# Score visits that wait for each bank pair on its own, and a down-projection in 512 columns

## The chip, the cores and the metric

The kernel runs on one core of a Trainium2 chip. The metric is device time in microseconds (us), the median of several executions. Engines are named as in the profile: PE is TensorE's matmuls and PEld its weight loads, DVE is VectorE, ACT is ScalarE, POOL is GpSimd, SP is SyncE, which issues the DMAs.

## The reference

One transformer block over x of 2048 tokens by 1024 features: attention with 32 query heads of width 32 that share one key and one value head, then a gated feed-forward part of width 3584, each behind a layer norm and with a residual.

```python
q = (ln(x) @ wq) as 32 heads of 32;  k = ln(x) @ wk;  v = ln(x) @ wv
p = softmax(q k^T * 32**-0.5)            # no mask: 2048 x 2048 for each head
h = x + concat_heads(p @ v) @ wo
g, u = ln(h) @ w_gate, ln(h) @ w_up      # 3584 columns each
out = h + (sigmoid(g) * u) @ w_down
```

All inputs and the output are bf16. `ln` is a layer norm without scale or shift.

## The kernel before

**A planner writes the order.** The kernel's Python first builds a plan. Class `Plan` keeps a list of operations for each engine, with an estimate of when each is ready, how long it holds its engine (`occ`) and when its result is there (`lat`, or for a DMA an estimate from its bytes and a constant, `late`). TensorE's list is written by one loop that looks, at each estimated moment, for what is ready. The other engines take the ready operation with the best priority. The lists are then emitted as they stand; real semaphores guard each true dependence, and a wait is left out when the engine has already waited for as high a value. So an engine runs its list strictly in order, whatever the real times are. The dictionary `TUNE` holds the constants of the planner: `late` and `pace` for DMAs, `parts1` for the number of attention parts of the second half tile, `eb` and `eq` for the choice between ACT and DVE when a result leaves PSUM, `pv_few` and `d_off`, `d_b` for when attention and down-projection work may be taken up.

**Score visits.** Attention goes over half tiles `hf` (128 tokens and 16 heads; 32 of them) and key tiles `kt` (128 keys; 16 of them): 512 visits, numbered v. In a visit four matmuls run in four row strips of the array at once (K is 32), each of 512 columns (4 heads by 128 queries), into four PSUM banks of `S_ps`. Those six banks are three pairs, used in rotation. Two exps follow on ACT, numbered u = 2v and 2v+1, each over 1024 columns of one pair, into a half of a slot of `Pr` (L701 in the profile). A visit v writes the pairs that exps 2v-3 and 2v-2 have read. `s_ready` gives what a visit waits for, `emit_S` writes it, and `choose` picks the half tile in the first 32 visits. Before the change all four matmuls wait for exp 2v-2, which comes after 2v-3 on the same engine, and both exps wait for the last of the four matmuls:

```python
            if v >= 1:
                deps.append(exps[2 * v - 2])
```

**The rest of the attention.** `mk_PV` multiplies the exps by V, in column strips of the array: a round of four matmuls (four groups of heads) runs at once, and 16 key tiles make 16 rounds for a half tile, in two or more parts. DVE adds each part into `oun` (L797, L801) and adds the exps up in `acc` (L676); `mk_SUM` sums those over the keys, and the reciprocal goes out to DRAM and comes back spread over the partitions (`rb`). `mk_OP` is the output projection, 16 matmuls a tile.

**The feed-forward part** of a tile of 128 tokens: `mk_GU`, seven groups of 512 columns, each one gate group and one up group of 8 matmuls into one bank of `F_ps`; a tanh on ACT (L983) and a product on DVE (L1004) make the activation, which a DMA transposes into `hact`. `mk_D` is the down-projection, 28 matmuls (3584 = 28 x 128) for each slice of the 1024 output columns. With `nd=4` there are four slices of 256 columns for each tile; DVE adds each slice to the residual (L1051). Gate and up weights are streamed from DRAM again for each tile, in slabs of 1 MB, into a ring of four slabs. For the first and the last tile the weights are the stationary side, and the matmuls have 128 columns.

All matmul groups other than the visits share the two banks of `F_ps`; a group can start when the eviction of the group before it in that bank is done. A visit is put between the matmuls of such groups whenever `s_ready` says it can begin and ACT has less than `run` = 700 ns of work left. The array has three modes here: row strips (visits), column strips (attention times V, sums) and dense (the rest). On DVE, short evictions have priority over the adds of L676.

Nearly all matmuls have the line number L445, that of a helper, so the profile tells them apart by their tiles: `S_ps<-QTb,kT` is a visit, `F_ps<-Pr,Vt` is exp times V, `F_ps<-acc,sel` a sum, `F_ps<-ring,hnT` gate or up, `F_ps<-zone,hact` the down-projection, `F_ps<-wo_sb,OT` the output projection.

Of the kernel before, what the change touches and what calls it, by code (L numbers as in the profile page):

```python
# [9 lines left out]
ACTF = mybir.ActivationFunctionType  # L10
# [5 lines left out]
SEM = 75.0  # L16


TUNE = dict(look=500, ln_v=1, warm=70, late=400, ws0=1, ws1=1, parts0=3, parts1=3, lord=2, h_ord=2, ho=3,
            ho2=0, pvl1=0, pvl2=0, col_ok=0, pace0=310, swait=400, parts=2, raw=1, rl=0, nd=4, pc=16, rate=315,  # L20
            pace=250, xd=4, qf=1, dall=1, wo_late=1, nkn=3, few=0, rmin=900, hmin=1, h0=100, h1=250, hf=1.35,
            run=700, sum_few=0, pv_few=3, d_off=1, d_a=-1, d_b=0, eb=700, eq=400)


class Op:
# [16 lines left out]
class Plan:  # L42
# [53 lines left out]
    def start_of(self, o):  # L96
# [4 lines left out]
        if o.eng == "dve" and o.prio >= 6:  # L101

            for p in self.heap["dve"]:
                if p.prio < 6 and s < p.ready < s + TUNE["look"]:
                    return p.ready
        return s

    def step(self, limit):
# [21 lines left out]
        if o.nbytes:  # L130
            if o.pace:
                self.pace_free = s + o.nbytes / TUNE["pace0" if self.fast(s) else "pace"]
            k = o.key.rstrip("0123456789_")
            go = max(s + 1720.0, self.dma_free)
            w = self.SLOW.get(k, 1.0) if k != "ha" else 2.5 if o.nbytes < 200000 else 1.3
            self.dma_free = go + o.nbytes * w / TUNE["rate"]
            o.end = self.dma_free + 700.0 + self.LATE.get(k, 0.0) + TUNE["late"]
        else:
# [20 lines left out]
def t_act(n):  # L159
    return dict(occ=n / 1.2 + 58.0, lat=n / 1.2 + 186.0 + SEM)  # L160
# [9 lines left out]
def bass_sequential_preLN__grouped_kv_mqa__glu_gated_glu__prompt_kernel(  # L170
# [19 lines left out]
    SCALE = 1.0 / math.sqrt(DH)  # L190
# [11 lines left out]
    with ExitStack() as es:  # L202
# [66 lines left out]
        pl = Plan()  # L269
# [45 lines left out]

        for c in ["xxqxxqxxxxxxqxxxxq", "qxqxxqxqxxxxxxxxxx", "xqxqxqqxxxxxxxxxxx", "xqxqxqxqxxxxxxxxxx", "xxqxqxqxqxxxxxxxxx"][TUNE["lord"]]:
            if c == "x":
# [19 lines left out]
        def stats(ph, tiles, srcs, deps, prio, after=((), ())):  # L337
# [8 lines left out]
            for t, src, dp in zip(tiles, srcs, deps):  # L346
# [14 lines left out]
                      occ=90, lat=250)  # L361
            if ph and TUNE["ln_v"] or not ph and t0 < 2:

# [80 lines left out]
        def mm(o, l, r, start, stop, **kw):  # L444
            return lambda: PE.matmul(o, lhsT=l, rhs=r, start=start, stop=stop, **kw)  # L445

        def pe_op(fn, n, mode, deps, last_of_round=True):
            if mode != pl.pe_mode:
                pl.free["pe"] += SWITCH
                pl.pe_mode = mode  # L450
            if mode == "dense":
                occ = max(25.0, n / 2.4 + 2.4)
            else:
                occ = max(25.0, n / 2.4 + 2.4) - 10.5 if last_of_round else 3.5
            return pl.op("pe", fn, deps, occ=occ, lat=max(25.0, n / 2.4 + 2.0) + 170.0 + SEM)
# [171 lines left out]
        def choose(v, t):  # L627

            cand = sorted((nxt[h], h) for h in range(2) if nxt[h] < NT)
            for kt, h in cand:  # L630
                visits[v] = (h, kt)
                sd = s_ready(v)
                if sd is not None and known(sd, t):
                    return
            visits[v] = cand[0][::-1]

        exps = {}
# [9 lines left out]
        def s_ready(v):  # L647
            hf, kt = visits[v]
            c, hh = hf // 2, hf % 2
            if any(2 * hh + k not in q_ready[c] for k in range(2)) or kt not in k_ev or not free_slots:  # L650
                return None
            deps = [q_ready[c][2 * hh], q_ready[c][2 * hh + 1], k_ev[kt]]
            if v >= 1:
                deps.append(exps[2 * v - 2])
            return deps

        late_adds = collections.defaultdict(list)
        RAW = tuple(range(TUNE["raw"])) + ((NH - 1,) if TUNE["rl"] else ())
# [2 lines left out]
        def make_add(hf, kt):  # L661

            pred = hf - 2
            if pred >= 0 and pred not in RAW and pred not in sum_last:
                late_adds[hf].append(kt)
                return
            a = acc[:, hf % 2, :]
            slot = slot_of[(hf, kt)]
            dp = [exp_of[(hf, kt, i)] for i in range(2)]
            if kt == 1:  # L670
                in0 = slot_of[(hf, 0)]
                dp += [exp_of[(hf, 0, i)] for i in range(2)] + [sum_last.get(pred)]
            else:
                in0 = a
                dp.append(add_op[(hf, kt - 1)])
            add_op[(hf, kt)] = pl.op("dve", lambda: DVE.tensor_tensor(out=a, in0=in0, in1=slot, op=ALU.add), dp, prio=6,  # L676
                                     occ=1135, lat=1255)
# [5 lines left out]
        def emit_S(v):  # L683
            hf, kt = visits[v]
            c, hh = hf // 2, hf % 2
            if hf < 2:
                nxt[hf] += 1
            deps = s_ready(v)
            last = None
            for j in range(4):  # L690
                bank = 2 * ((2 * v + j // 2) % NB) + j % 2
                last = pe_op(mm(S_ps[:, bank, :], kT4[DH * j:DH * (j + 1), kt * P:(kt + 1) * P],
                                QTb[DH * j:DH * (j + 1), (c // 2) % 2, 4 * hh:4 * hh + 4, (c % 2) * P:(c % 2 + 1) * P],
                                True, True, tile_position=(DH * j, 0)),
                             512, "row", deps if j == 0 else [], j == 3)
            slot, rel = free_slots.popleft()
            slot_of[(hf, kt)] = slot
            for i in range(2):
                u = 2 * v + i
                pb = 2 * (u % NB)  # L700
                exps[u] = pl.op("act", lambda i=i, pb=pb: ACT.activation(  # L701
                    out=slot[:, i * 1024:(i + 1) * 1024].rearrange("p (a b) -> p a b", a=2), in_=S_ps[:, pb:pb + 2, :],
                    func=ACTF.Exp, scale=SCALE), [last] + rel, prio=3, **t_act(1024))
                exp_of[(hf, kt, i)] = exps[u]
            if kt >= 1 and hf not in RAW:
                make_add(hf, kt)
            if hh == 1 and c % 2 == 1 and kt == NT - 1:
                pair_last_S[c // 2] = last
                load_q(c // 2 + 2)
            if kt + 1 in parts_of(hf):  # L710
                if kt == NT - 1 and hf not in RAW:
                    queues["SUM"].append(mk_SUM(hf))
                queues["PV"].append(mk_PV(hf, parts_of(hf).index(kt + 1) - 1))
                if hf in RAW:
                    queues["PV"].append(mk_PV(hf, parts_of(hf).index(kt + 1) - 1, True))
# [3 lines left out]
        def parts_of(hf):  # L719
            return PARTS[TUNE["parts" if hf > 1 else "parts0" if hf == 0 else "parts1"]]  # L720
# [353 lines left out]
        cur = None  # L1074
        cur_i = 0
        cur_b = None
        v = 0
# [3 lines left out]
        def all_done(v):  # L1081

            v_done[0] = v
            if v == NV:
                all_S[0] = True
                pl.t_last = pl.free["pe"]
                load_next([(s.rearrange("p (d f) -> p d f", d=4), rel) for s, rel in free_slots])

        def known(deps, t):
            return all(d is not None and d.end is not None and d.end <= t for d in deps)  # L1090

        while True:
            t = pl.free["pe"]
# [14 lines left out]
            if v < NV:  # L1108
                run = max(pl.free["act"], t) + sum(o.occ for o in pl.heap["act"])
                if v < 2 * NT:  # L1110
                    choose(v, t)
                sd = s_ready(v)
                can_s = sd is not None and known(sd, t)
                if can_s and run - t < TUNE["run"]:
                    emit_S(v)
                    v += 1
                    all_done(v)
                    idle = 0
                    continue
                if pl.pe_mode == "col" and sd is not None and not can_s and not (  # L1120
                        cur is not None and cur[1][cur_i][2] != "dense") and known(sd, t + TUNE["swait"]) and run - t < TUNE["run"] + TUNE["swait"]:

                    pl.free["pe"] = t + 25.0
                    continue
            else:
                can_s = False
            if cur is not None and not held and cur[0].cls in LONG and known(bank_rel[1 - cur_b], t):

                for cl in ("PV", "SUM", "OP", "hT"):
                    if queues[cl] and (v >= NV or len(free_slots) <= TUNE["few"] or cl == "PV" and pl.pe_mode == "row" or (  # L1130
                            len(cur[1]) - cur_i) * max(25.0, cur[1][cur_i][1] / 2.4 + 2.4) >= TUNE["rmin"]):
                        gr = queues[cl][0]
                        if (gr.gate is None or gr.gate()) and known(gr.first(), t):
# [3 lines left out]
                            cur = (gr, gr.atoms(cur_b), list(bank_rel[cur_b]) + gr.first())  # L1137
                            cur_i = 0
                            break
            if cur is not None:  # L1140
                at = cur[1][cur_i]
                if known(at[3], t):
# [7 lines left out]
                    if cur_i == len(cur[1]):  # L1150
                        bank_rel[cur_b] = cur[0].after(cur_b, o)
                        cur = None
                        if held:
                            cur, cur_i, cur_b = held.pop()
                    idle = 0
                    continue
            else:
# [14 lines left out]
                if pick is not None:  # L1172
# [4 lines left out]
                    cur = (gr, gr.atoms(b), list(bank_rel[b]) + gr.first())  # L1177
                    cur_i, cur_b = 0, b
                    continue
            if can_s:  # L1180
                emit_S(v)
                v += 1
                all_done(v)
                continue
# [113 lines left out]
```

## Time and profile before

| | |
|---|---|
| time, median of 3 | 1097.02 us (1096.5 to 1098.07) |
| span of the profiled execution | 1098.3 us |
| granted TensorE clock | 0.998 of full speed |
| exps: 1024, mean length | 949.3 us busy for 1008 of them, 1120 ns each |
| tanhs: 112 | 75.4 us, 673 ns each |
| down-projection matmuls: 1792 | 224.3 us, 273 ns each |
| gate and up matmuls of 512 columns: 1439 recorded | 357.5 us, 380 ns each |

How to read it: an engine's instructions overlap, the end of one with the start of the next, so the mean length of one is not the spacing between two. An exp lasts 1120 ns and yet 1008 of them are busy for 949.3 us in all. Spacing is read from starts in the timeline. Some matmul records are missing in the trace, so a count of 1439 stands for more.

### The profile page before, as it was taken

The numbers are of one execution on the slowest core, as the hardware profiler recorded it, in microseconds if no ns is written. First come the engines' busy times: TensorE is split into PE (matmuls) and PEld (weight loads), VectorE is DVE, ScalarE is ACT, GpSimd is POOL, SyncE is SP. The second block draws the span as 40 slices with busy tenths as digits, with TensorE's granted clock in tenths as the row PEclk, the third lists the DMA queues.
The fourth block names the chain that finished last, engine by engine and source line by source line (L and its number), as shares of the span: only waits on it lengthen the run. The fifth ranks groups of instructions, "written<-read, shape, count | busy, mean of one in ns | idle before, by whom it ended". The sixth has DMA issues, their size and how long they took to land.

```text
span 1098.3 us, 25235 instructions
## 1 busy us (share of the span) xinstructions
PE 1062.8 (97%) x10227; PEld 529.1 (48%) x10350; DVE 851.6 (78%) x1087; ACT 1003.4 (91%) x1151; POOL 39.5 (4%) x61
## 2 busy tenths in 40 slices
PE   7999989999999999999999999999999999999999
PEld 6533465444444444444444444444444444444598
DVE  7988988787878878787878878787887878787311
ACT  4999999999999999999999999999999999999010
POOL 3300000000000000000000000000000000000000
PEclk9999999999999999999999999999999999999999
DMA  8793598958869595968868595877859595886993
GB/s 247 146 319 97 134 309 274 271 140 259 224 177 255 141 271 145 258 174 241 235 167 257 141 267 151 257 190 213 254 148 260 136 259 155 245 216 176 284 310 109
DMA packets 296515, 233.80 MB, mean 213 GB/s; under 512 B 99536, under 2 KB 282832, under 8 KB 296400
## 3 DMA queue, kind: packets, MB, share of 16 engines
q1 hardware_dynamic: 296400, 232.19, 76.1%
q8 instruction: 82, 1.34, 0.5%
q14 instruction: 33, 0.27, 0.1%
HBM read 203.82 MB, written 8.12 MB: 193 GB/s over the span
## 4 chain that ended last, share of the span: by engine, by line
PE 46%; ACT 42%; issue 4%; DVE 4%; DMA 3%; SPq 1%; POOL 0%; DVEq 0%
PE F_ps L445 39%; ACT Pr L701 38%; PE S_ps L445 7%; ACT tnh L983 3%; DVE acc L676 2%; DMA rb<-r_scratch 1%; DMA ring<-in_A_x_dram 1%; DMA ring<-in_B_w_up_dram 1%; SPq L303 0%; SPq L745 0%; DMA r_scratch<-r_sb 0%; ACT hact L701 0%; ACT QTb L701 0%; DVE h_sb L1051 0%; SPq L312 0%
## 5 line engine op out<-in xcount | busy, mean ns | idle before, releaser
L701 ACT ACTIVATE Pr<-S_ps 128x1024 bf16<-128x1024 f32 x1008 | 949.3, 1120 | 4.6 <-PE S_ps L445 4.4
L676 DVE TENSOR_TENSOR acc<-acc,Pr 128x2048 bf16<-128x2048 bf16 x430 | 524.6, 1220 | 72.3 <-ACT Pr L701 59.8
L445 PE MATMUL F_ps<-ring,hnT 128*128 128x512 bf16 x1439 | 357.5, 380 | 11.2 <-issue 9.2
L445 PE MATMUL F_ps<-zone,hact 128*128 128x256 bf16 x1792 | 224.3, 273 | 0.1
L445 PEld LDWEIGHTS F_ps<-ring,hnT 128*128 128x128 bf16 x1536 | 131.4, 97 | 176.2 <-issue 58.6
L445 PE MATMUL S_ps<-QTb,kT 32*128 32x512 bf16 x2048 | 202.4, 385 | 8.2 <-ACT Pr L701 2.9
L445 PEld LDWEIGHTS F_ps<-zone,hact 128*128 128x128 bf16 x1792 | 166.3, 98 | 51.9 <-issue 21.1
L445 PEld LDWEIGHTS S_ps<-QTb,kT 32*128 32x128 bf16 x2048 | 51.5, 91 | 183.5 <-ACT Pr L701 141.8
L445 PE MATMUL F_ps<-Pr,Vt 128*32 128x512 bf16 x2016 | 136.2, 382 | 0.0
L983 ACT ACTIVATE tnh<-F_ps 128x512 f32<-128x512 f32 x112 | 75.4, 673 | 61.0 <-PE F_ps L445 44.8
L1004 DVE SCALAR_TENSOR_TENSOR act_s<-tnh,F_ps 128x512 bf16<-128x512 f32 x98 | 67.0, 684 | 24.1 <-PE F_ps L445 23.6
L445 PE MATMUL F_ps<-zone 128*128 128x512 bf16 (+3 forms) x573 | 73.8, 272 | 6.0 <-DMA zone<-in_A_wq_dram 1.4
L445 PEld LDWEIGHTS F_ps<-Pr,Vt 128*32 128x32 bf16 x2016 | 46.5, 96 | 65.1 <-issue 30.5
L445 PE MATMUL F_ps<-wo_sb,OT 128*128 128x512 bf16 x243 | 61.8, 381 | 3.2 <-issue 1.9
L367 POOL TENSOR_TENSOR dsb<-zb,cst 128x1 bf16<-128x1 bf16 x18 | 23.0, 1278 | 968.4 <-DVE zb L364 968.4
L445 PEld LDWEIGHTS F_ps<-zone 128*128 128x128 bf16 x584 | 38.6, 97 | 33.8 <-issue 9.6
L1051 DVE SCALAR_TENSOR_TENSOR h_sb<-F_ps,h_sb 128x256 bf16<-128x256 f32 x64 | 26.9, 420 | 28.4 <-PE F_ps L445 28.3
L801 DVE TENSOR_TENSOR oun<-F_ps,oun 128x512 f32<-128x512 f32 x34 | 23.4, 689 | 25.9 <-PE F_ps L445 25.8
L445 PE MATMUL F_ps<-hnT,ring 128*128 128x128 bf16 x608 | 39.9, 223 | 1.5 <-DMA ring<-in_B_w_up_dram 0.8
L445 PEld LDWEIGHTS F_ps<-hnT,ring 128*128 128x128 bf16 x608 | 35.5, 100 | 7.4 <-issue 6.6
L797 DVE COPY oun<-F_ps 128x512 f32<-128x512 f32 x32 | 22.1, 691 | 21.7 <-PE F_ps L445 21.6
L676 DVE TENSOR_TENSOR acc<-Pr 128x2048 bf16<-128x2048 bf16 x31 | 37.0, 1193 | 0.1
(78 smaller groups left out, 351.0 us busy)
## 6 DMA issues: line engine op xcount, KB each, us to landing
ring<-in_B_w_gate_dram SPq DMA_DIRECT2D x308, 256.0 KB, 4.0
ring<-in_B_w_up_dram SPq DMA_DIRECT2D x308, 256.0 KB, 3.9
rb<-r_scratch SPq DMA_DIRECT2D x124, 64.0 KB, 2.6
zone<-in_B_w_down_dram SPq DMA_DIRECT2D x14, 512.0 KB, 4.9
Pr<-in_B_w_up_dram SPq DMA_DIRECT2D x20, 256.0 KB, 5.7
Pr<-in_B_w_gate_dram SPq DMA_DIRECT2D x20, 256.0 KB, 6.5
ring<-in_A_x_dram SPq DMA_DIRECT2D x16, 256.0 KB, 6.7
h_sb<-in_A_x_dram SPq DMA_DIRECT2D x16, 256.0 KB, 3.0
```

The lines of the kernel that those rows point to most:

```text
L367: g = pl.op("pool", lambda: POOL.tensor_tensor(out=dsb[:, ph, tk], in0=zb[:, ph, tk], in1=half[:, 0:k], op=ALU.pow), [f, c0], prio=0, **sl ...
L445: return lambda: PE.matmul(o, lhsT=l, rhs=r, start=start, stop=stop, **kw)
L676: add_op[(hf, kt)] = pl.op("dve", lambda: DVE.tensor_tensor(out=a, in0=in0, in1=slot, op=ALU.add), dp, prio=6, occ=1135, lat=1255)
L701: exps[u] = pl.op("act", lambda i=i, pb=pb: ACT.activation(out=slot[:, i * 1024:(i + 1) * 1024].rearrange("p (a b) -> p a b", a=2), in_=S_ ...
L797: oun_ev[(hf, 0)] = pl.op("dve", lambda: DVE.tensor_copy(out=o, in_=F_ps[:, b, :]), [last, ot_ev.get(hf - 2)], prio=0, **t_dve(512))
L801: oun_ev[(hf, part)] = pl.op("dve", lambda: DVE.tensor_tensor(out=o, in0=F_ps[:, b, :], in1=o, op=ALU.add), [last, oun_ev[(hf, part - 1)]] ...
L983: box["a"] = pl.op("act", lambda: ACT.activation(out=tnh[:, :], in_=F_ps[:, b, :], func=ACTF.Tanh, scale=0.5), [last, box.get("e")], prio= ...
L1004: e = pl.op("dve", lambda: DVE.scalar_tensor_tensor(out=so, in0=tnh[:, :], scalar=1.0, in1=F_ps[:, b, :], op0=ALU.add, op1=ALU.mult), [las ...
L1051: e = pl.op("dve", lambda: DVE.scalar_tensor_tensor(out=h_sb[:, t % NHB, sl], in0=F_ps[:, b, 0:DW], scalar=0.5, in1=h_sb[:, t % NHB, sl], ...
```

## The change

A visit's first two matmuls wait only for the exp that has to free their own pair (2v-3); the third waits for exp 2v-2. The first exp of a visit waits for the second matmul, the second exp for the fourth. The planner may put a visit up to `early` = 240 ns (by its own estimate) before exp 2v-2 ends. It is meant to let scores of a pair begin while the other pair is still being read. The down-projection goes from four slices of 256 columns to two of 512 (`nd=2`), so half as many matmuls and evictions. Eight other constants of the planner are changed with it (`late`, `parts1`, `pace`, `pv_few`, `d_off`, `d_b`, `eb` and `eq`), and since all operations are placed by estimate, the order on every engine changes.

```diff
-TUNE = dict(look=500, ln_v=1, warm=70, late=400, ws0=1, ws1=1, parts0=3, parts1=3, lord=2, h_ord=2, ho=3,
-            ho2=0, pvl1=0, pvl2=0, col_ok=0, pace0=310, swait=400, parts=2, raw=1, rl=0, nd=4, pc=16, rate=315,
-            pace=250, xd=4, qf=1, dall=1, wo_late=1, nkn=3, few=0, rmin=900, hmin=1, h0=100, h1=250, hf=1.35,
-            run=700, sum_few=0, pv_few=3, d_off=1, d_a=-1, d_b=0, eb=700, eq=400)
+TUNE = dict(early=240, look=500, ln_v=1, warm=70, late=300, ws0=1, ws1=1, parts0=3, parts1=4, lord=2, h_ord=2,
+            ho=3, ho2=0, pvl1=0, pvl2=0, col_ok=0, pace0=310, swait=400, parts=2, raw=1, rl=0, nd=2, pc=16,
+            rate=315, pace=265, xd=4, qf=1, dall=1, wo_late=1, nkn=3, few=0, rmin=900, hmin=1, h0=100, h1=250,
+            hf=1.35, run=700, sum_few=0, pv_few=4, d_off=0, d_a=-1, d_b=1, eb=450, eq=1500)
@@ s_ready
-            if v >= 1:
-                deps.append(exps[2 * v - 2])
+            if v >= 2:
+                deps.append(exps[2 * v - 3])
             return deps
+
+        def s_known(v, t):
+
+            sd = s_ready(v)
+            return sd is not None and known(sd, t) and (v < 1 or known([exps[2 * v - 2]], t + TUNE["early"]))
@@ emit_S
-                             512, "row", deps if j == 0 else [], j == 3)
+                             512, "row", deps if j == 0 else [exps[2 * v - 2]] if j == 2 and v >= 1 else [], j == 3)
+                if j == 1:
+                    mid = last
...
-                    func=ACTF.Exp, scale=SCALE), [last] + rel, prio=3, **t_act(1024))
+                    func=ACTF.Exp, scale=SCALE), [last if i else mid] + rel, prio=3, **t_act(1024))
@@ the loop that writes TensorE's list
-                sd = s_ready(v)
-                can_s = sd is not None and known(sd, t)
+                can_s = s_known(v, t)
```

The two other places where the loop and `choose` asked `s_ready` and `known` ask `s_known` instead.

More of the change, by code (lines that the diff above doesn't have):

```diff
@@ L631, in choose @@
                 visits[v] = (h, kt)
-                sd = s_ready(v)
-                if sd is not None and known(sd, t):
+                if s_known(v, t):
                     return
@@ L1111, in bass_sequential_preLN__grouped_kv_mqa__glu_gated_glu__prompt_kernel @@
                     choose(v, t)
-                sd = s_ready(v)
-                can_s = sd is not None and known(sd, t)
+                can_s = s_known(v, t)
                 if can_s and run - t < TUNE["run"]:
@@ L1119, in bass_sequential_preLN__grouped_kv_mqa__glu_gated_glu__prompt_kernel @@
                     continue
-                if pl.pe_mode == "col" and sd is not None and not can_s and not (
-                        cur is not None and cur[1][cur_i][2] != "dense") and known(sd, t + TUNE["swait"]) and run - t < TUNE["run"] + TUNE["swait"]:
+                if pl.pe_mode == "col" and not can_s and not (
+                        cur is not None and cur[1][cur_i][2] != "dense") and s_known(v, t + TUNE["swait"]) and run - t < TUNE["run"] + TUNE["swait"]:
                     pl.free["pe"] = t + 25.0
```

## Prediction

> **What bounds the kernel now.** I read the page's engine rows, then the slices, then windows of the steady part, then timelines of single engines there and of the end.
>
> ```profile
> PE 1062.8 (97%) x10227; PEld 529.1 (48%) x10350; DVE 851.6 (78%) x1087; ACT 1003.4 (91%) x1151; POOL 39.5 (4%) x61
> ACT  4999999999999999999999999999999999999010
> PE 46%; ACT 42%; issue 4%; DVE 4%; DMA 3%; SPq 1%; POOL 0%; DVEq 0%
> ```
>
> Two engines are nearly full, and the chain that ended last is split between them. The slices show two regimes: ScalarE (ACT) is solid up to slice 37, then only TensorE (PE) works, to the end. The windows (length; then busy time and count per engine) give the period of the steady part:
>
> ```profile
> 451.92:514.15 62.23, 60.97 (x553) 27.96 (x560) 50.26 (x60) 62.22 (x72) 1.45 (x1) 1.00 0.75 209
> 514.15:576.38 62.23, 60.97 (x553) 27.94 (x560) 50.46 (x60) 62.22 (x72) 1.45 (x1) 1.00 0.78 215
> ```
>
> One tile of 128 tokens takes 62.23 us, again and again. Busy shares can't say which engine sets it, because both kinds of instruction overlap their successors. Starts can. The ScalarE timeline (start, length):
>
> ```profile
> 522.61 0.63 ACT L983 ACTIVATE tnh<-F_ps 128x512 f32<-128x512 f32 x1
> 523.09 7.49 ACT L701 ACTIVATE Pr<-S_ps 128x1024 bf16<-128x1024 f32 x8
> 530.31 0.75 ACT L983 ACTIVATE tnh<-F_ps 128x512 f32<-128x512 f32 x1
> ```
>
> Eight exps take 530.31 - 523.09 = 7.22, so 0.903 each, though one lasts 1.12; a tanh takes 523.09 - 522.61 = 0.48. A tile has 64 exps and 7 tanhs: 57.8 + 3.4 = 61.1 us. So ScalarE has about 1.1 us to spare in 62.23.
>
> TensorE, from the same timelines: 112 gate/up matmuls and 16 of the output projection at 0.216 (27.6), 112 down-projection matmuls at 0.109 (12.2), 32 visits at 0.226 (7.2), 33 rounds of attention-times-V at 0.216 (7.1), two sums (0.5), and 70 changes of array mode at about 0.10 (6.8). With 0.01 lost on the matmul after each visit this is 61.8 us. TensorE is therefore the slightly tighter engine. What it loses beyond is in these lines:
>
> ```profile
> 501.09 1.69 PE L445 MATMUL F_ps<-Pr,Vt 128*32 128x512 bf16 x26
> 502.71 0.39 PE L445 MATMUL S_ps<-QTb,kT 32*128 32x512 bf16 x4
> ...
> 547.70 1.48 PE L445 MATMUL F_ps<-Pr,Vt 128*32 128x512 bf16 x24
> 549.11 0.40 PE L445 MATMUL S_ps<-QTb,kT 32*128 32x512 bf16 x4
> ```
>
> 26 matmuls take 502.71 - 501.09 = 1.62 to the next visit, 24 take 1.41. Four of them run at once, so a visit that cuts a round in two pays a second pass: 0.21 us. That is the 33rd round. Then a wait for a bank:
>
> ```profile
> 518.65 0.69 DVE L801 TENSOR_TENSOR oun<-F_ps,oun 128x512 f32<-128x512 f32 x1 [1.38 <-PE F_ps L445]
> 519.66 0.59 PE L445 MATMUL F_ps<-ring,hnT 128*128 128x512 bf16 x2 [0.39 <-DVE oun L801]
> ```
>
> Right after the sums a gate group needs the bank that the attention part still holds; it costs TensorE about 0.25 us a tile. What is not there: in the steady part hardly any visit waits for an exp. Visits start 0.11 to 0.87 us after exp 2v-2 has ended, where a visit that really waits (in the first 60 us) starts 0.054 after it. The 142 us that the waits table puts to "PEld S_ps <- ACT Pr" are mostly weight loads that stand behind a mode change.
>
> After the last visit, at 1012, TensorE works for 83 us alone while the weights stream in:
>
> ```profile
> 1012.00:1030.00 18.00, 17.34 (x158) 9.74 (x160) 7.03 (x10) 3.76 (x5) 0.00 (x0) 1.00 1.00 279
> 1030.00:1045.00 15.00, 14.72 (x93) 8.79 (x94) 5.43 (x14) 1.19 (x2) 0.55 (x1) 1.00 1.10 286
> 1045.00:1062.00 17.00, 16.24 (x262) 15.59 (x260) 3.14 (x5) 2.39 (x4) 0.00 (x0) 1.00 1.08 306
> ```
>
> DMA share is 1 there: the queues are full, and the end could become theirs.
>
> **What the Trainium skill says.** "TensorE: Matmul & The Clock Gate", section Back-to-back issue gap, gives N/2.4 + 2.5 ns: 216 for 512 columns, 109 for 256. The starts agree (0.216, 0.109). "TensorEngine Tiling (Array Packing)", Key Properties, says a change of tiling mode drains the array; here each change costs about 0.10. "Perfetto Trace Analysis", Tensor Engine Instruction, puts semaphore waits in a queue ahead of the execution FIFO. The trace agrees for dense work: matmuls that carry a satisfied wait start 0.216 after the one before, as those without. No row of this trace shows a wait inside a burst of four. "Per-tile semaphore tail" of the first page prices an increment at about 26 ns, on the way to the waiting engine.
>
> **The change, part by part**, using the order in which the changed kernel's instructions stand.
>
> (1) Start on the free pair, wait inside. The first two matmuls of a visit wait only for exp 2v-3, the third for exp 2v-2. Behind that third matmul stands everything on TensorE's queue. If TensorE comes early by d, it used to idle d before four matmuls; now two run and the array waits d before the other two. The end is the same. If it comes late, both waits are over. So the steady gain is nearly nothing. The cost of the added wait lies between 0 (as in dense work) and 0.216 (the second pair streams alone). I take 0, as visits here are late by 0.06 us or more.
>
> (2) Each exp on its own pair. Exp 2v can start 7 ns earlier (two starts 3 to 4 ns apart), and ScalarE is busy with exp 2v-1 then. The extra increment's 26 ns are hidden by that exp too. Nothing.
>
> (3) Down-projection in 512 columns: 1792 x 0.1092 = 195.7 becomes 896 x 0.2158 = 193.4 on TensorE: -2.2 us. On DVE 64 evictions of 0.42 become 32 of about 0.69, 26.9 to 22 us; DVE is 78% busy and off the path, except the very last eviction: +0.27.
>
> (4) The new constants move the order. Counted in it: runs in one array mode go from 1135 to 1168, in a steady tile from 70 to 73 changes: 33 x 0.097 = +3.2 us. Cut attention rounds go from 15 to 4: -11 x 0.216 = -2.4 us. After the sums no gate group follows; the down-projection, which already holds its bank, goes on. The bank wait leaves: 13 tiles x 0.25 = -3.2 us. The shortest stretches of TensorE work between visits now follow each other (1.61, 1.72, 1.84 us against 1.81 of exps), so TensorE may run ahead and wait there for exps: I allow 0.07 a tile, +0.9.
>
> (5) DMA is trusted 0.1 us more and paced 6% faster. The same 656 weight pieces move. Gate/up groups now come in runs of 24 or 32 matmuls, up to four slabs back to back from a ring of four. Taken as hidden: three quarters of the steady DMA waits of before end over 3.8 us before their matmul. After the last visit the work at the prices above is 79.9 us against 80.8; that is part of the sums, not added. The waits for weights there stay as they are (about 2 us).
>
> (6) The first 200 us hold some 18 us of TensorE waits, at the start and around the first finished tile. The new order has the same shortage there (stretches of 1.02 and 0.23 us where there were 1.02 and 0.65). Nothing, plus or minus 2 us.
>
> Sum: -2.2 + 0.27 + 3.2 - 2.4 - 3.2 + 0.9 = -3.4. 1097.0 - 3.4 gives 1093.6 us.
>
> **The rivals.** *The wait inside costs TensorE time.* Against: satisfied waits are free in dense work. For: four matmuls start within 10 ns, so anything at the third is exposed, and 800 visit matmuls carry a wait instead of 512. If one visit in ten lost the whole second pass, 51 x 0.216 = +11 us: 1104.6; at 20 ns for each of 511, +10: 1103.8. Slower.
>
> *Weights come late.* For: four slabs in about 8.5 us is over 450 GB/s from the ring, against 209 to 215 on average; pacing is tighter. Against: the ring refills while attention runs. At 0.25 a tile, 13 x 0.25 = 3.3 us: the gain is gone, 1096.9.
>
> *The beginning improves too.* If a third of those 18 us go, because evictions and visits stand differently there, 1093.6 - 6 = 1087.6. For: ScalarE still idles there. Against: the shortage in (6).
>
> **How the numbers follow.** My forecast 0.55, the wait inside 0.15, late weights 0.18, a better beginning 0.12. The predicted time is the first, 1093.6. Faster by over 0.2% (below 1094.8): most of the first, all of the last: 0.65. Within: late weights and the upper edge of the first: 0.20. Slower: 0.15. The range reaches from near the better beginning, 1087, to 1100, half of the cost of the wait inside; the full cost, 0.1 or so, stays out.
>
> **What would show it.** Right: a steady tile of about 62.0 us, no split rounds, no bank wait after the sums, 0.216 from down-projection start to start, third visit matmul 3 ns after the second nearly always. Wrong: gaps between the second and third matmul, TensorE waits on slabs in the runs of gate/up, a tile of 62.2 or more, or a beginning that shifts by more than 2 us.

## The result and the profile after

The changed kernel takes 1092.54 us (median of 4, 1092.28 to 1094.73), the kernel before 1097.13 beside it (4 runs): ratio 0.9962, 95% interval [0.9945, 0.9979]. A repeat gave 0.9962 [0.9949, 0.9974]. The forecast was 1093.6.

The page of the changed kernel, the same rows as before: engines, slices of ScalarE, chain that ended last, and the row of the new eviction in 512 columns (busy us, mean ns of one).

```profile
PE 1060.6 (97%) x9314; PEld 439.3 (40%) x9454; DVE 848.9 (78%) x1054; ACT 1000.7 (92%) x1152; POOL 39.5 (4%) x61
...
ACT  4999999999999999999999999999999999999010
...
ACT 67%; PE 22%; issue 5%; DVE 3%; DMA 2%; SPq 0%; DVEq 0%
...
L1057 DVE SCALAR_TENSOR_TENSOR h_sb<-F_ps,h_sb 128x512 bf16<-128x512 f32 x32 | 22.1, 692 | 40.4 <-PE F_ps L445 40.3
```

The shares tell almost nothing: 97% and 92% where 97% and 91% were. The chain's swing to ACT (42% to 67%) is no proof either, since with two engines this close a few nanoseconds decide which one is followed back. But it points the right way, as ScalarE's timeline shows further down.

Windows of two steady tiles (length; busy and count per engine):

```profile
461.65:523.75 62.10, 60.90 (x497) 22.19 (x504) 50.00 (x57) 62.10 (x72) 1.45 (x1) 1.00 0.75 215
523.75:585.84 62.09, 60.89 (x497) 22.19 (x504) 49.78 (x57) 62.09 (x72) 1.46 (x1) 1.00 0.74 207
```

A tile takes 62.10 where it took 62.23, as regularly. Next, what TensorE waited for (us in total, times, longest us) in eight tiles. Before, from 452 to 949 us:

```profile
PE F_ps L445 <- issue: 6.5, 31, 0.4
PE F_ps L445 <- DVE OT L759: 0.7, 1, 0.7
PE F_ps L445 <- DVE oun L801: 0.4, 1, 0.4
```

After, from 461 to 958 us:

```profile
PE F_ps L445 <- issue: 6.2, 39, 0.2
PE S_ps L445 <- ACT Pr L707: 2.0, 8, 0.3
PE F_ps L445 <- DVE acc L680: 0.2, 1, 0.2
```

Most of these rows are not waits. A window above counts 504 weight loads and 497 matmuls: seven matmul records a tile are missing, and where a missing matmul is the first after a change of array mode, the gap that it leaves is listed as "issue", 0.16 long (6.2 / 39 in the new kernel). The rows of 0.4 before hold such a gap and a real wait: for the bank after the sums, mostly without a named releaser. The weight loads give its length. The first gate load came 0.56 after the sums began, where a group whose bank is free comes 0.35 after them (518.06 to 518.41 in the new kernel), so the wait was 0.21:

```profile
518.86 0.42 PE L445 MATMUL F_ps<-acc,sel 128*32 128x64 bf16 x32
519.41 0.34 PEld L445 LDWEIGHTS F_ps<-ring,hnT 128*128 128x128 bf16 x3 [0.26 <-issue]
```

It has left. The row "S_ps <- ACT Pr" of the new kernel, once in each tile (2.0 / 8 = 0.25), is again a missing matmul, of the down-projection: its weights were loaded at 515.57. The place itself, in the timeline (start, length):

```profile
515.57 0.10 PEld L445 LDWEIGHTS F_ps<-zone,hact 128*128 128x128 bf16 x1 [0.42 <-issue]
515.90 0.41 PE L445 MATMUL S_ps<-QTb,kT 32*128 32x512 bf16 x4 [0.26 <-ACT Pr L707]
516.24 1.47 PE L445 MATMUL F_ps<-zone,hact 128*128 128x512 bf16 x6
517.64 0.50 PE L445 MATMUL S_ps<-QTb,kT 32*128 32x512 bf16 x4
518.07 0.42 PE L445 MATMUL F_ps<-acc,sel 128*32 128x64 bf16 x32
518.41 1.25 PE L445 MATMUL F_ps<-zone,hact 128*128 128x512 bf16 x4
```

After the sums (518.07) the down-projection goes on at once in a bank it already holds. The visit at 517.64 lasts 0.50 instead of 0.39: its second pair started 109 ns after the first. This is the change's early start at work, about twice in a steady tile: the visit at 515.90 is split by 14 ns. So TensorE waits about 0.12 a tile for exps.

Why it waits shows in ScalarE's timeline:

```profile
521.05 2.15 ACT L707 ACTIVATE Pr<-S_ps 128x1024 bf16<-128x1024 f32 x2
522.90 0.79 ACT L989 ACTIVATE tnh<-F_ps 128x512 f32<-128x512 f32 x1
523.37 3.98 ACT L707 ACTIVATE Pr<-S_ps 128x1024 bf16<-128x1024 f32 x4
527.08 0.76 ACT L989 ACTIVATE tnh<-F_ps 128x512 f32<-128x512 f32 x1
527.56 4.87 ACT L707 ACTIVATE Pr<-S_ps 128x1024 bf16<-128x1024 f32 x5
```

Read it from the ends (start plus length), since it is the end of an exp that a visit waits for. The tanhs end at 523.69 and 527.84, each 0.49 after the exp before it; the nine exps after them take 3.66 + 4.59, so 0.917 each. In the single records of this steady tile every exp ends 0.916 to 0.918 after the instruction before it, although the starts of consecutive exps lie 0.904 to 1.022 apart: a start that comes later by 0.1 does not make the end later. And in none of the fourteen profiles of this case do two exps in a row end less than 0.912 apart. 64 x 0.9165 + 7 x 0.49 = 62.09. ScalarE has no time to spare in the new tile; it sets it. Before, by the same count, one exp in each steady tile ended 0.114 late and a few others by 0.02 or less, 0.14 in all. That is the difference between 62.23 and 62.09.

By stage, from the profiled executions (spans 1098.3 and 1092.9, so -5.4; the medians differ by 4.6). In both of them the granted clock dips once, near 146 us (last section); two experiments without that dip stand beside them, 4 with the old order and 1 with the new:

| stage | before | after | experiment 4 | experiment 1 |
|---|---|---|---|---|
| to visit 96 | 203.27 | 202.08 | 201.26 | 201.00 |
| visits 96 to 511 | 808.78 | 805.17 | 808.21 | 805.18 |
| from the last visit to the end | 86.23 | 85.65 | 84.77 | 84.59 |

Most of the gain is in the middle stage (3.6 of 5.4, and 3.0 of 3.5 from experiment 4 to 1). Its 830 exps and 91 tanhs take 805.4 us at the spacings above. In the new kernel ScalarE's ends fall behind that by 0.07 us in the whole stage, before by 3.3. Twelve whole tiles lie in it. Before, three of them are much longer (63.06, 62.43, 62.41); after, all but the first two are 62.096 or 62.097.

### The profile page after: what moved, and what is told of

It is laid out like the page before. It is cut to its first block, busy times and chain, and to the rows that moved or that the text cites. A ratio compares the mean times of both kernels' runs of the same rounds, so it can differ in the third digit from the quotient of the medians.

```text
span 1092.9 us, 23470 instructions
## 1 busy us (share of the span) xinstructions
PE 1060.6 (97%) x9314; PEld 439.3 (40%) x9454; DVE 848.9 (78%) x1054; ACT 1000.7 (92%) x1152; POOL 39.5 (4%) x61
## 4 chain that ended last, share of the span: by engine, by line
ACT 67%; PE 22%; issue 5%; DVE 3%; DMA 2%; SPq 0%; DVEq 0%
ACT Pr L707 62%; PE F_ps L445 19%; ACT tnh L989 5%; PE S_ps L445 3%; DVE acc L680 1%; DMA hnT<-hn 1%; DMA r_scratch<-r_sb 1%; DMA zone<-ring 0%; DVE st L349 0%; DVE st L351 0%; DMA ring<-in_A_x_dram 0%; DMA rb<-r_scratch 0%; DVE hact L285 0%; DVE ring L393 0%; DVE OT L765 0%
## 5 line engine op out<-in xcount | busy, mean ns | idle before, releaser
L445 PE MATMUL F_ps<-ring,hnT 128*128 128x512 bf16 x1506 | 366.8, 380 | 4.4 <-issue 4.1
L445 PE MATMUL F_ps<-zone,hact 128*128 128x512 bf16 x813 | 212.1, 381 | 6.5 <-issue 4.3
L445 PE MATMUL S_ps<-QTb,kT 32*128 32x512 bf16 x2048 | 206.8, 385 | 5.6 <-ACT Pr L707 4.7
L445 PEld LDWEIGHTS F_ps<-ring,hnT 128*128 128x128 bf16 x1536 | 134.6, 98 | 180.8 <-issue 43.0
L989 ACT ACTIVATE tnh<-F_ps 128x512 f32<-128x512 f32 x112 | 83.7, 747 | 60.3 <-PE F_ps L445 60.3
L445 PEld LDWEIGHTS F_ps<-zone,hact 128*128 128x128 bf16 x896 | 75.5, 97 | 104.0 <-issue 34.6
L445 PEld LDWEIGHTS F_ps<-Pr,Vt 128*32 128x32 bf16 x2016 | 43.0, 95 | 68.0 <-issue 28.6
L1057 DVE SCALAR_TENSOR_TENSOR h_sb<-F_ps,h_sb 128x512 bf16<-128x512 f32 x32 | 22.1, 692 | 40.4 <-PE F_ps L445 40.3
L445 PEld LDWEIGHTS F_ps<-wo_sb,OT 128*128 128x128 bf16 x256 | 21.3, 97 | 34.0 <-issue 12.5
```

What stands on the lines that cost most here:

```text
L989: box["a"] = pl.op("act", lambda: ACT.activation(out=tnh[:, :], in_=F_ps[:, b, :], func=ACTF.Tanh, scale=0.5), [last, box.get("e")], prio= ...
L1057: e = pl.op("dve", lambda: DVE.scalar_tensor_tensor(out=h_sb[:, t % NHB, sl], in0=F_ps[:, b, 0:DW], scalar=0.5, in1=h_sb[:, t % NHB, sl], ...
```

## The experiments

Ratios are to the kernel before, in runs on the same chip, with 95% intervals. "List" is TensorE's work counted from the instruction order, at the durations measured in the trace of before; it holds no waits. The new waits need not be planned to be tried: semaphore dependences can be changed after the planner has fixed the order, and the order then stays the same instruction for instruction.

**1. The changed kernel again**, as the yardstick. 

> The changed kernel once more, as the yardstick of this set. Both theories: 1092.5 us, 4.5 below the kernel before, a steady tile of 62.10 us.

Measured 1092.29 us, 0.9962 [0.9949, 0.9974]; tile 62.097, visits 96 to 511 805.17.

**2. New order, old waits** (`quad` holds the four matmuls of visit v; the lines stand after the planning).

```diff
+        for v, quad in vis:
+            if v >= 1:
+                quad[0].deps.append(exps[2 * v - 2])
+                quad[2].deps.remove(exps[2 * v - 2])
+            exps[2 * v].deps[0] = quad[3]
```

> The changed kernel's order on every engine, with the waits of before put back: all four matmuls of a visit wait for exp 2v-2, both exps for the fourth matmul. Theory (the gain is the order and the 512 columns; the waits are worth almost nothing): 1092.5 to 1094.5, a steady tile of 62.1 to 62.2 us, the one visit a tile that was split by 109 ns now late by about the same. Rival (the waits make the gain): about 1097, a steady tile of 62.4 or more.

Measured 1092.85 us, 0.9966 [0.9953, 0.9978]; tile 62.097, visits 96 to 511 805.20. The early start and the exp on its own pair together are worth nothing that can be told apart. No visit is split here (38 are in the changed kernel), and exps that wait for their visit start 435 ns or more after its last matmul, where it is 419 in the changed kernel.

**3. New order, only the start waits old**: the last line of that diff left out. 

> As the run with the old waits, but each exp follows its own pair. Theory: within 1 us of the changed kernel; the first exp of a late visit starts about 420 ns after the visit's last matmul started, as in the changed kernel, where it was 437 before. Rival (starting on the free pair is what counts): 1096 or more.

Measured 1091.74 us, 0.9959 [0.9947, 0.9972]; tile 62.097, visits 96 to 511 805.18. Each late exp starts about 16 ns sooner here than in experiment 2 (419 against 435), and the tile is the same to a nanosecond. This is no evidence that TensorE sets the tile: the exps start sooner and don't end sooner. In both runs the exps of a steady tile end 0.914 to 0.919 apart, and the tile is what 64 exps and 7 tanhs take. Old or new, the waits leave ScalarE full in this order, so they can't matter to the tile.

**4. Old order, new waits**: the mirror of experiment 2, in the kernel before.

```diff
+            if v >= 1:
+                quad[0].deps.remove(exps[2 * v - 2])
+                quad[2].deps.append(exps[2 * v - 2])
+            if v >= 2:
+                quad[0].deps.append(exps[2 * v - 3])
+            exps[2 * v].deps[0] = quad[1]
```

> The order of the kernel before on every engine, with the new waits: two matmuls wait for exp 2v-3, the third for 2v-2, each exp for its own pair. Theory: 1096 to 1097, a steady tile of 62.1 to 62.23 us, the cut rounds and the bank wait still there. Rival (the waits make the gain): about 1092.5. Second rival (a wait inside the visit costs TensorE time): 1099 or more, with 10 ns or more between the second and third matmul in most visits.

Measured 1096.74 us, 0.9995 [0.9987, 1.0003]; tile 62.23, as before. Its waits of TensorE from 451 to 948 us:

```profile
PE F_ps L445 <- issue: 3.8, 24, 0.2
PE F_ps L445 <- DVE oun L805: 3.1, 8, 0.4
PE F_ps L445 <- DVE OT L763: 0.5, 1, 0.5
```

Here the bank wait after the sums is named: the eviction into `oun`, once in each of the eight tiles (of the 0.39 a part is again a missing record). So the order makes the gain, and the bank wait goes with the order.

**5. 512 columns alone**, in the kernel before.

```diff
-nd=4
+nd=2
```

> The kernel before with the down-projection in 512 columns, nothing else; the planner then writes another order. Priced as in the prediction (streams, 1170 runs in one array mode at 0.097, 6 cut rounds at 0.216) TensorE's list is 1061.6 us, where it is 1062.3 before and 1061.0 in the changed kernel. Theory (the order's price on TensorE, plus 31 to 35 us of waits that all these kernels have, is the time): 1093 to 1096.5. Rival (512 columns are worth more than their 2.2 us, as DVE and PSUM get freer): 1092.5 or less.

Measured 1097.46 us, 0.9997 [0.9989, 1.0005]: nothing, and 1 us above what the theory had allowed. TensorE's cheaper matmuls are there, but the planner, with its other constants as they were, writes an order in which tiles take from 61.70 to 62.99 us, with two cut attention rounds in some and waits for exps in others. Visits 96 to 511 take 810.29.

**6. The changed kernel with 256 columns** (`nd=2` to `nd=4`, nothing else). 

> The changed kernel with the down-projection in 256 columns again. Its TensorE list is priced 1064.6 us (1180 runs in one mode, 5 cut rounds), 3.6 above the changed kernel. Theory: 1095.5 to 1099. Rival (the waits and constants make the gain, the columns none): 1092.5 to 1093.

Measured 1099.13 us, 1.0020 [1.0013, 1.0028], slightly above its range: 6.8 us over the yardstick, for matmuls that cost 2.3 us more. Steady tile 62.31, some of 63.2 and more (three waits for `OT`, 1.9 us together).

**7. The changed kernel with the old trust in DMAs.**

```diff
-late=300
-pace=265
+late=400
+pace=250
```

> The changed kernel with the DMA estimates of before (late 400, pace 250). The planner's order has 1182 runs in one mode and 30 cut attention rounds; its TensorE list is priced 1068.1 us, 7 above the changed kernel. Theory: 1099 to 1103, slower than before, with two cut rounds in each steady tile. Rival (weights that come late are what these constants act on): 1092 or less if the old trust is safer, with the cut rounds costing nothing.

Measured 1098.98 us, 1.0018 [1.0011, 1.0025], a hair under its range. The list has 30 cut attention rounds in all (two in a steady tile, 0.216 each by the price in the prediction), and the tile is 62.57, 0.48 over what ScalarE needs. No weights come late. These two constants act through the order alone: 6.7 us, more than the whole change.

**8. All constants of after in the kernel before**: its `TUNE` replaced by that of the changed kernel (`nd=2` among them), the visits' code untouched. 

> The kernel before with all constants of the changed one, 512 columns among them, but the waits of before, also in the planner. Its TensorE list is priced 1059.6 us (1155 runs in one mode, 4 cut rounds), 1.4 below the changed kernel. Theory: 1091 to 1094.5, so at least as fast as most of the changed kernel's gain. Rival (waiting for each pair on its own is needed for the gain): 1096 or more.

Measured 1101.10 us, 1.0033 [1.0020, 1.0046]: a clear miss. The number lies in the rival's range, but not for the rival's reason, as experiment 2 has the old waits too. The steady tile is 62.12, about what ScalarE needs. But the time from the last visit to the end was 91.1 us, where the changed kernel has 85.65. The windows show why (second to last figure: DMA share; last: GB/s). First this kernel, from its last visit on:

```profile
1008.20:1040.00 31.80, 31.51 (x201) 13.66 (x200) 12.66 (x21) 4.78 (x7) 0.55 (x1) 1.00 1.05 280
1040.00:1060.00 20.00, 16.74 (x244) 14.29 (x244) 3.44 (x5) 2.69 (x5) 0.00 (x0) 1.00 1.10 308
1060.00:1080.10 20.10, 20.10 (x208) 13.74 (x207) 2.76 (x4) 1.49 (x3) 0.00 (x0) 1.00 0.95 313
1080.10:1099.30 19.20, 16.24 (x131) 9.38 (x128) 2.76 (x4) 0.60 (x1) 0.00 (x0) 1.00 0.06 21
```

Then the changed kernel:

```profile
1007.30:1040.00 32.70, 30.99 (x196) 13.58 (x199) 13.22 (x22) 4.97 (x7) 0.55 (x1) 1.00 0.99 293
1040.00:1057.00 17.00, 16.32 (x241) 14.29 (x243) 2.06 (x3) 2.39 (x4) 0.00 (x0) 1.00 1.06 296
1057.00:1074.10 17.10, 17.05 (x198) 12.60 (x198) 2.76 (x4) 1.20 (x2) 0.00 (x0) 1.00 0.90 291
1074.10:1092.90 18.80, 15.76 (x122) 8.99 (x121) 2.76 (x4) 0.60 (x1) 0.00 (x0) 1.00 0.06 22
```

In both the DMA queues are full until the last weights land (1080.1 and 1074.1), and 19 us of work follow. The kernel of experiment 8 issues 72 pieces of 256 KB after its last visit, the changed kernel 65. In the second window TensorE idles 3.3 us (20.00 - 16.74); the waits from the last visit on have it as

```profile
PE F_ps L445 <- DMA Pr<-in_B_w_up_dram: 2.8, 1, 2.8
PE F_ps L445 <- DMA Pr<-in_B_w_gate_dram: 0.4, 1, 0.4
```

So the plan had put work off until after the last visit (83.7 us of list against 80.1), and its weights had to come there.

**9. One constant more, in the changed kernel.**

```diff
-sum_few=0
+sum_few=1
```

> The changed kernel with one constant moved (the sums may stand straight after a visit): TensorE's list at the measured durations is 1059.04 us (1060.10 in the changed kernel), but 83.5 us of it stand after the last visit (79.9). The theory that the whole list sets the time: 1092.4 - 1.06 = 1091.3 us (1090.5 to 1092). The rival, that work put off until after the last visit is paid twice, because its weights must then come through queues that are already full: 3.6 us more work in the tail brings about 7 more pieces of weights of 256 KB, at some 300 GB/s 6 us of transfers, of which TensorE waits for 2 to 4: 1094 to 1098 us.

Measured 1099.12 us, 1.0021 [1.0014, 1.0027]: slower, as the rival said, though by a little more than its range. The list is shorter by 1.06 us, but the tail is 90.3 us, again with 72 pieces of weights. The steady tile is a test of the bound: it has 72 changes of mode where the changed kernel has 73, so TensorE's list for it is 0.10 shorter, yet it takes the same 62.096 or 62.097 from exp end to exp end. TensorE waits about 0.22 in it instead of 0.12. Shortening TensorE's list there gains nothing, because ScalarE has no time left.

**10. The counterpart of experiment 8**: the changed kernel with the constants of before (`early` stays). 

> The changed kernel with all its planning constants set back to those of before (down-projection in 256 columns among them); the visits keep their new waits. It is the counterpart of the kernel of before with the constants of after. TensorE's list at the measured durations is 1.7 us longer than the changed kernel's, but 7.5 us more of it stand after the last visit and 5.8 us less ahead of it. If the whole list sets the time: 1092.4 + 1.7 = 1094.1 us (1093 to 1095.5). If the weights that are still to come after the last visit set the tail, at about 1 us for a piece (72 pieces issued after the last visit took 71.3 and 71.9 us to the last landing in two runs, 65 took 66.8, 55 took 56.7) and 19 us from the last landing to the end: 7.5 us of work are about 14 pieces more than the changed kernel's 65, so the last visit at 1007.3 - 5.8 = 1001.5, the last landing 79 us later, and the end at 1099.5 us (1097 to 1102). If the new waits are worth something by themselves: below 1093.

Measured 1106.45 us, 1.0078 [1.0064, 1.0092], above both ranges. The tail is 94.2 us, with 76 pieces. The last landing came 77 us after the last visit and the end 17 us later, close to the 79 and 19 expected; but the last visit came at 1012.2, not at 1001.5. Visits 64 to 96 tell why: their list is 54.2 us, short by the work that was put off, and they take 66.4. In those 66.5 us TensorE and ScalarE show

```profile
137.90:204.40 66.50, 62.25 (x753) 33.67 (x750) 54.90 (x61) 63.45 (x73) 0.56 (x1) 0.92 0.83 251
```

ScalarE is busy for 63.45 us, exactly as long as in the 64.70 us that the changed kernel takes for these visits. Work that TensorE puts off here saves no time, since the exps have to be done all the same; it is paid in full at the end. (The granted clock was 0.92 in this stretch and 0.97 in the changed kernel's, so part of the 66.5 may be the clock's.)

**11 and 12. A search for a version that beats both.** Orders with a shorter list *and* a shorter tail come from planning visits later: `run=500` with `eq=400`, and `run=400`.

```diff
-run=700
-eq=1500
+run=500
+eq=400
```

> The changed kernel with two constants moved: a visit is planned only when ScalarE's planned work reaches less than 500 ns ahead (700 in the changed kernel), and the bias of one kind of eviction is 400 as before the change. TensorE's list at the measured durations is 1056.65 us (1060.10 in the changed kernel: 35 fewer changes of array mode), and what stands after the last visit is 65.2 us of it (79.9). The theory that TensorE's list, with the same few waits, sets the time: the list is 3.45 us shorter, 1092.4 - 3.45 = 1089.0 us (1088 to 1090.5), the tile about 63.0 and the tail about 71, as work has moved from behind the last visit to ahead of it. The rival that a wait takes over: ScalarE gets its visits later, and the weights are wanted faster while attention runs, so TensorE's waits for slabs grow; 1092 us or more, with a tile over 63.2.

Measured 1166.13 us, 1.0629 [1.0613, 1.0645]. The other one, `run=700` to `run=400` alone:

> The changed kernel with one constant moved: a visit is planned only when ScalarE's planned work reaches less than 400 ns ahead (700 in the changed kernel). TensorE's list at the measured durations is 1055.88 us (1060.10), 65.2 us of it after the last visit (79.9). If TensorE's list with the same waits sets the time: 1092.4 - 4.2 = 1088.2 us (1087 to 1090). If ScalarE, which is then given its work with 300 ns less in hand, idles so that the visits end later than the list says, or TensorE waits for weights or evictions instead: 1092 us or more.

Measured 1202.04 us, 1.0959 [1.0932, 1.0986]. The rival holds, and how much it costs was not foreseen. In the first of the two, the list after the last visit was indeed short (the tail fell to 75.4 us), but a tile takes 65.8 to 71 us. Lines of its timeline of TensorE:

```profile
428.07 0.75 PE L445 MATMUL S_ps<-QTb,kT 32*128 32x512 bf16 x6
429.58 0.39 PE L445 MATMUL S_ps<-QTb,kT 32*128 32x512 bf16 x2 [0.76 <-ACT Pr L707]
430.55 0.60 PE L445 MATMUL F_ps<-ring,hnT 128*128 128x512 bf16 x2 [0.59 <-DMA ring<-in_B_w_up_dram]
```

Two visits stand back to back; the second begins on its free pair and then waits 0.76 for the other, and the next gate/up group waits for its weights. 59 visits are split, by 37 us in all. From visit 192 on, the list of these tiles (61 to 62 us) is hardly longer than the changed kernel's; the waits between are, at 4.4 to 9.6 us a tile. Part of the loss may be the clock's: in the profiled execution it was at half for some 41 us, which can cost TensorE at most half of that, of 78 us over experiment 1.

## Why the prediction was right, point by point

It was right about the order and wrong about the bound. It called TensorE "the slightly tighter engine" and gave ScalarE "about 1.1 us to spare", from eight exps whose starts lie 0.903 apart. The same lines, read from the ends, say something else: the tanh ends at 523.24 (522.61 + 0.63) and the eight exps at 530.58 (523.09 + 7.49), 0.917 each. ScalarE needs 62.09 us for a tile and had 0.14 to spare, not 1.1. ("Spacing is read from starts" held for TensorE only.) TensorE with its bank wait did set the old tile, at 62.23; ScalarE sets the new one. That the tile came out near the predicted "about 62.0" is luck to this extent: ScalarE's limit happens to lie just there, and an order that saved TensorE twice as much would have gained no more in the steady tiles. No experiment changed ScalarE's own work, so its limit is read from the traces: counted from exp end to exp end, no tile of any profile takes less than its exps and tanhs at those spacings, and the steady tiles of experiments 1, 2, 3 and 9, with two orders and three sets of waits, all stop at 62.096 or 62.097.

(1) **Start on the free pair, wait inside: 0.** Confirmed in both orders: 1092.85 without it against 1092.29 with it in the new order, and in the old order 1096.74 with it, at 0.9995 [0.9987, 1.0003]. The bound of 0.216 a visit was far off. What the Trainium skill says under "Perfetto Trace Analysis", Tensor Engine Instruction, of waits held in a queue ahead of execution fits inside a burst of four too: the third matmul starts 3 to 4 ns after the second whenever its wait is over. The prediction expected that nearly always; 474 of 512 visits do, and the 38 split ones come about twice a steady tile.

(2) **Each exp on its own pair: nothing.** Right in effect, wrong in size: a waiting exp starts about 17 ns earlier, not 7. Its end is no earlier in the steady tile of the new order, where ScalarE is full.

(3) **512 columns: -2.2 us on TensorE.** The term is fair as a price (its factors give -2.3; eviction 692 ns, as taken), but it can't be had alone: experiment 5 gained nothing, and experiment 6 lost 6.8. The slices' length moves the whole order in both cases.

(4) **The order.** Terms per steady tile: list up by 0.15 (512 columns -0.15, three more changes of mode +0.29), less the 33rd round, which is gone (-0.22). The bank wait is gone (0.25 predicted, 0.21 by the weight loads). The wait for exps is the term that was mis-sized: 0.07 allowed, 0.12 measured, and it is what ScalarE's limit leaves over. That adds up to -0.16; measured is -0.133, and the other 0.03 was not traced. So the predicted "about 62.0" was 62.10, and the thirteen tiles gave -1.7 us of the order's gain. (TensorE's sum for the old tile, given as 61.8, comes to 61.7 from the terms listed.)

What made up for it was not foreseen, and is luck for the number: the three longer tiles of before, 1.2 us together, and 0.65 in the first tiles and the last stretch of the stage. In the old order two runs of two have longer tiles. All lose their time at the same visit of the tile, the longest to a wait of 0.5 or 0.7 for `OT`, the product that follows the round trip of the reciprocal. In four runs of the new order (with the old or the new waits) there is none. Step (5) had only the weights in view. Experiment 6 has such waits again, so it is this order and not the new code that avoids them; why was not tried. Together visits 96 to 511 gave -3.6 us.

(5) **DMA: nothing, tail -0.9 in the list.** The tail fell by 0.6 in the profiled pair and by 0.2 from experiment 4 to 1, less than it differs between runs of one order (84.5 to 85.7 in the four runs of the new one). So nothing was lost there, and a gain isn't shown. It was nearer an edge than the prediction said: full queues were foreseen, but not that seven more pieces in the tail (experiments 8 and 9) cost 4.6 to 5.5 us over the changed kernel's 85.65.

(6) **The beginning: nothing, plus or minus 2.** This held: -1.2 in the profiled pair, both with a dip of the clock there, and -0.25 from experiment 4 to experiment 1, both without.

The rivals: the wait inside costing TensorE time is refuted by experiments 2 to 4. Weights late in the steady part: not seen in the changed kernel. A better beginning: 0.25 to 1.2 of the 6 us that it assumed.

What stays open: experiments 8 to 10 show that constants and code have to be tuned together (1092.5 with both, 1101.1 and 1106.5 with one), but not which of the eight constants does what, except the DMA pair and `nd`.

## What to carry to other kernels

When a planner writes the order, a change to a wait or a tile size is two changes: fix the order and change the wait alone, then fix the wait and change the order. Here the wait named in the title was worth nothing, and the order, with the 512 columns in it, all of the 4.6 us. When two engines are close, size the slack of the second from where its instructions end, over a whole period: read from starts, ScalarE's slack seemed 1.1 us and was 0.14, and once that was used up no shorter list for TensorE could help the steady part. And ask where removed work went: work moved behind the last overlap is paid again in transfers, and work given late to the second engine stalls the first.

## What the runs showed of the hardware

On ScalarE, exps of 128x1024 from PSUM in the changed kernel's steady tile end 0.916 to 0.918 us apart, in no profile less than 0.912. They last 1.02 to 1.33 (kernel before, all its exps), so one starts well before the one ahead of it ends, and starts can lie as close as 0.903 for several exps in a row. Starts taken from such a row overstate the rate. A visit that waits for an exp starts 0.054 to 0.055 us after that exp's end.

In some executions the granted TensorE clock falls to half for 3.4 us. In the changed kernel's profile it is this window (the figure before the DMA share is the clock):

```profile
145.50:148.90 3.40, 3.40 (x59) 2.67 (x52) 3.30 (x4) 2.24 (x3) 0.00 (x0) 0.51 1.06 342
```

The new order has a dip at the same place in experiment 2 and none there in experiments 1 and 3, with spans of 1092.9 and 1092.9 against 1090.8 and 1090.8. Over more executions the difference is smaller: of the kernel before, beside experiments 5 to 8, 12 executions with a mean clock of 0.998 have a median of 1098.0 us, and 32 with 1.000 have 1096.9. Such a dip, in a stretch where TensorE had been waiting for exps, thus goes with 1 to 2 us, up to half the effect under study; that it causes them isn't shown. In the profiled executions of experiments 11 and 12, where TensorE waits often, there are five or more of them, up to 13.7 us long.
